# Linear attention with a SwiGLU feed-forward on one core: reordering batch 0's exponentials, cutting dummy matmuls, and merging batch 1's second products

## The chip, the cores and the metric

The kernel runs on one core of a Trainium2 chip. The metric is the device time of one execution in microseconds (us). Each kernel was executed several times; a time given alone is the median, with the lowest and highest beside it where they matter. The profile is one traced execution. Its "span" is 1.7 to 1.8 us shorter than the time of the same execution in every run of this study (315.0 us against a span of 313.2, 314.28 against 312.5). All runs quoted here are in the fast state.

## The reference

```python
def _attn_ref(q, k, v):                      # (8, 8, 576, 64) each: batch, head, sequence, head_dim
    def phi(x):
        return np.where(x > 0, x, np.exp(x) - 1.0) + 1.0
    q_p, k_p = (phi(q), phi(k))
    kv = np.einsum('bhsd,bhse->bhde', k_p, v)
    z = np.sum(k_p, axis=2)
    num = np.einsum('bhsd,bhde->bhse', q_p, kv)
    den = np.einsum('bhsd,bhd->bhs', q_p, z)[..., None] + 1e-06
    return num / den

def _moe_ref(x, w_gate, w_val, w_out):       # 4608 tokens, 512 -> 1536 -> 512
    g = x @ w_gate
    silu = g * (1.0 / (1.0 + np.exp(-g)))
    return (silu * (x @ w_val)) @ w_out
```

The attention's output, with the heads side by side, is the feed-forward's input x. The large work is the feed-forward, on PE (TensorE).

## The kernel before

Tokens are processed in periods of 512. One period is layer 1 (products with w_gate and w_val; two lines, L276 where the first chunks are taken in an order of their own, and L292 elsewhere) and layer 2 (products with w_out, L299). All operands are fp16, sums are fp32. Attention is hidden beside this, except for batch 0, which must be done before layer 1 can begin, and for the end of batch 1, which lies inside layer 2 of the first period.

Attention of one batch goes like this. phi of k is built as max(k, 0) + min(exp(k), 1): `exp_k` on ACT (ScalarE), `mx_k`, `mn_k` and `add_k` on DVE (VectorE). `q_exp` and `q_phi` do the same for batch 0's transposed q. `zt` sums phi(k) over the sequence on PE (L398), `zr_copy` spreads the sum, and `t_corners` with `Zr` is the q.z block (L254), the denominator. `lnrd` makes the reciprocal on ACT as exp(-ln). `kv_corner` is the product of phi(k) and v (L185), copied to `R`. `t_corners` with `R` is the q.R block (L254 again), the numerator. `x_t` multiplies numerator and reciprocal on DVE into `xT`, layer 1's input. A "dummy" (`warm`, L124) is a matmul on ones that nothing uses; it keeps PE active while it waits.

```python
WARM = (4, 1, 4, 5, 2, 1, 2, 2)              # how many dummies at each of eight places
...
def warm(n, w=512, ps=None):
    for _ in range(n):
        nc.tensor.matmul(out=(ps or pp4[1][1])[:, 512 - w:512], lhsT=ones[:, :],
                         rhs=ones[:, 0:1].to_broadcast([P, w]), start=True, stop=True)
...
# batch 0, cut: order of issue; each engine executes its own instructions in this order
q_turn(1, qb)                                # PE: transposes of q's second half
q_exp(1, 0, qb)                              # ACT
q_exp(1, 1, qb)                              # ACT
warm(WARM[2])
exp_k(0, 0)                                  # ACT
exp_k(0, 1)
q_phi(0, 0, qa)                              # DVE
q_phi(0, 1, qa)
mx_k(0, 0)
q_phi(1, 0, qb)
q_phi(1, 1, qb)
mn_k(0, 0)                                   # DVE, needs the first exp_k
zt(0, 0, X[1], kp, True, False)              # PE: z of half 0, part of max(k, 0)
warm(WARM[3])
zt(0, 0, X[1], ek, False, True)              # PE: z of half 0, part of min(exp(k), 1)
zr_copy(0, 0, X[1])
warm(WARM[4])
t_corners(0, Zr, 0, pp4[2])                  # PE: q.z block
lnrd(pp4[2], 0)                              # ACT: ln, exp
...
warm(WARM[6])
kv_corner(0, 0, kp, True, True)              # PE: products of v
...
warm(WARM[7], ps=pp4[2][1])
l1_mm(0, 0, pp4[2], (0,))                    # PE: first products of layer 1
l1_mm(0, 1, X, (0,))
t_corners(0, R, 1, pp4[1])                   # PE: second q.R block
x_t(0, 1, pp4[1])                            # DVE
...
# layer 2 of the first period, cut: its last part, with the end of batch 1
s4()                                         # den(0), den(1): q.z blocks and reciprocals of batch 1
for t in range(4):
    if t == 2:
        for lp in range(2):
            kv_corner(1, lp, kp, True, True)
        r_copy(1, 0, 2, "VV")
    if t == 3:
        nx(0, dz)                            # PE: q.R block, DVE: x_t
    for fb in range(FO, FB):
        l2_mm(0, t, fb)                      # PE: layer 2
    if t < 3:
        l2_out(0, t, "V")                    # DVE: copy of an output tile (L322)
nx(1, cq)
...
# layer 1 of the second period, cut
for cs in ((0, 1), (2, 3)):                  # chunks of x, two at a time
    for i in range(2):
        l1_mm(g, i, two[i], cs)
```

Of the kernel before, what the change touches and what calls it, by code (L numbers as in the profile page):

```python
# [9 lines left out]
AF = mybir.ActivationFunctionType  # L10
# [7 lines left out]
def kernel(  # L18
# [21 lines left out]
    EPS = 1e-6  # L40
    SC = 4096.0
    NB = 3
    WARM = (4, 1, 4, 5, 2, 1, 2, 2)

    sb = ctx.enter_context(tc.tile_pool(name="sb", bufs=1))
    pp = ctx.enter_context(tc.tile_pool(name="ps", bufs=1, space=bass.MemoryType.PSUM))
# [2 lines left out]
    def many(shape, dt, name, n=2):  # L49
        return [sb.tile(shape, dt, name=f"{name}_{i}") for i in range(n)]  # L50
# [12 lines left out]
    rd = many([P, 2, 512], FP16, "rd")  # L63

    q32 = sb.tile([P, HL, J * D], FP32, name="q32")
    lnt = many([P, 512], FP32, "lnt", 4)
# [19 lines left out]
    epsb = sb.tile([P, 1], FP32, name="epsb")  # L86
# [32 lines left out]
    def act(out, in_, func=AF.Copy, scale=1.0, bias=0.0):  # L119
        nc.scalar.activation(out=out, in_=in_, func=func, bias=bias, scale=scale)  # L120
# [5 lines that stand above are left out]
# [4 lines left out]
    def jl(t, b, lp):  # L130
        return t[b % 2][:, lp, :, :].rearrange("p j (l d) -> p l j d", d=D)

    def lj(t, b, lp):
        return t[b % NB][:, hs(lp), :].rearrange("p l (j d) -> p l j d", d=D)

    def exp_k(b, lp):
        act(jl(ek, b, lp), lj(kr, b, lp), AF.Exp)
# [4 lines left out]
    def mx_k(b, lp):  # L142
        nc.vector.tensor_scalar(out=jl(kp, b, lp), in0=lj(kr, b, lp), scalar1=0.0, scalar2=None, op0=ALU.max)

    def mn_k(b, lp):
        a = ek[b % 2][:, lp, :, :]
        nc.vector.tensor_scalar(out=a, in0=a, scalar1=1.0, scalar2=None, op0=ALU.min)  # L147
# [31 lines left out]
    def kv_corner(b, lp, t, first, last):  # L179
        ps = kvp[b]  # L180
        for j in range(J):
            for l2 in range(2):
                for hh in range(2):
                    rows = slice(C * hh, C * hh + C)
                    nc.tensor.matmul(out=ps[hh][D * l2:D * l2 + D, D * lp:D * lp + D],  # L185
                                     lhsT=t[b % 2][rows, lp, j, D * l2:D * l2 + D],
                                     rhs=vr[b % NB][rows, 2 * lp + l2, D * j:D * j + D],
                                     start=(first and j == 0), stop=(last and j == J - 1))
# [113 lines left out]
    def l2_open(g, t):  # L302
        if t % 2 == 0:
            l2p[(g, "p", t // 2)] = pair()
        l2p[(g, t)] = l2p[(g, "p", t // 2)][t % 2]
# [90 lines left out]
    def zt(b, lp, ps, t, first, last):  # L396
        for j in range(J):
            nc.tensor.matmul(out=ps[:, 0:2], lhsT=t[b % 2][:, lp, j, :], rhs=ob[:, 0:P:C],  # L398
                             start=(first and j == 0), stop=(last and j == J - 1))

    def zr_copy(b, lp, ps):
        nc.vector.tensor_scalar(out=Zr[b][:, lp, :, :], in0=ps[:, 0:2].unsqueeze(2).to_broadcast([P, 2, D]),
                                scalar1=1.0 / SC, scalar2=None, op0=ALU.mult)

    def lnrd(ps, i, w0=0, w1=512, early=False):
        for l2 in range(2):
            act(lnt[2 * i + l2][:, w0:w1], ps[l2][:, w0:w1], AF.Ln, bias=epsb[:, 0:1])
            if not early:
                act(rd[i][:, l2, w0:w1], lnt[2 * i + l2][:, w0:w1], AF.Exp, scale=-1.0)
        for l2 in range(2 if early else 0):  # L410
            act(rd[i][:, l2, w0:w1], lnt[2 * i + l2][:, w0:w1], AF.Exp, scale=-1.0)

    def xmul(dst, ps, r):
        nc.vector.scalar_tensor_tensor(out=dst, in0=ps, scalar=1.0 / SC, in1=r, op0=ALU.mult, op1=ALU.mult)

    def x_t(g, lp, ps, l2s=(0, 1)):
        for l2 in l2s:
            xmul(xT[g % 2][:, 2 * lp + l2, :], ps[l2][:, :], rd[lp][:, l2, :])

    def t_corners(g, W, lp, ps):  # L420
        for (b, j0, j1, c0) in units(g)[1]:
            corners(ps, W[b], b, lp, j0, j1, c0)

    def q_one(pair_):
        for h in range(2):
            nc.tensor.matmul(out=pair_[h][:, :], lhsT=part[:, :], rhs=ones[:, 0:1].to_broadcast([P, 512]),
                             start=True, stop=False)

    def q_turn(lp, pair_):
        for l2 in range(2):  # L430
            for j in range(J - 1):
                nc.tensor.matmul(out=pair_[j // 4][D * l2:D * l2 + D, P * (j % 4):P * (j % 4) + P],
                                 lhsT=qr[0][:, 2 * lp + l2, D * j:D * j + D], rhs=id16[:, :],
                                 start=False, stop=(j % 4 == 3))

    def q_half(lp, h):
        return qT[0][:, lp, 4 * h:4 * h + 4, :, :].rearrange("p j h c -> p (j h c)")

    def q_exp(lp, h, pair_):
        act(q_half(lp, h), pair_[h][:, :], AF.Exp, bias=m1[:, 0:1])  # L440

    def q_phi(lp, h, pair_):
        a = q_half(lp, h)
        nc.vector.scalar_tensor_tensor(out=a, in0=pair_[h][:, :], scalar=1.0, in1=a, op0=ALU.max, op1=ALU.min)  # L444

    kvp[0] = pp4[1]
    X = [pp4[0][0], pp4[3][0]]
    Y = [pp4[3][1], pp4[0][1]]
    qa, qb = pp4[2], pp4[0]
# [3 lines left out]
    nc.vector.tensor_copy(out=qr[0][:, 3, :], in_=q32[:, 3, :])  # L453
    warm(WARM[0])
    q_one(qa)
# [3 lines left out]
    q_exp(0, 1, qa)  # L459
    warm(WARM[1])  # L460
    q_turn(1, qb)
    q_exp(1, 0, qb)
    q_exp(1, 1, qb)
    warm(WARM[2])
    exp_k(0, 0)
    exp_k(0, 1)
    q_phi(0, 0, qa)
    q_phi(0, 1, qa)
    mx_k(0, 0)
    q_phi(1, 0, qb)  # L470
    q_phi(1, 1, qb)
    mn_k(0, 0)
    zt(0, 0, X[1], kp, True, False)
    warm(WARM[3])
    zt(0, 0, X[1], ek, False, True)
    zr_copy(0, 0, X[1])
    warm(WARM[4])
    t_corners(0, Zr, 0, pp4[2])
    lnrd(pp4[2], 0)
    mx_k(0, 1)  # L480
    mn_k(0, 1)
    zt(0, 1, Y[0], kp, True, False)
    warm(WARM[5])
    zt(0, 1, Y[0], ek, False, True)
# [6 lines left out]
    r_copy(0, 0, 1, "VV")  # L491
    add_k(0, 1)
    t_corners(0, R, 0, X)
    x_t(0, 0, X, (0,))
    kv_corner(0, 1, kp, True, True)
    x_t(0, 0, X, (1,))
    r_copy(0, 1, 2, "VV")
    warm(WARM[7], ps=pp4[2][1])
    l1_mm(0, 0, pp4[2], (0,))
# [20 lines left out]
    def p1_open():  # L520
        b1p["z"] = kvp[1] = pair()
        ring.pop()
        b1p["q"] = pair()
        ring.pop()
# [54 lines left out]
    def layer2_0():  # L579
        for t in range(4):  # L580
            l2_open(0, t)
        p1_open()
        cq, dz = b1p["q"], b1p["z"]
        nc.scalar.preload_act_table_set("natural_log_exp_and_others")

        def den(lp, ps):
            t_corners(1, Zr, lp, ps)
            lnrd(ps, lp, early=(lp == 0))

        def nx(lp, ps):  # L590
            t_corners(1, R, lp, ps)
            x_t(1, lp, ps)

        def s0():
            act(eq[0][:, :, D * 8:D * 9], qr[0][:, :, D * 8:D * 9], AF.Exp)
            exp_k(1, 1)
            exp_q(1, 0)
            exp_q(1, 1)
            phi_q8()
            mx_p(0)  # L600
            mn_k(1, 1)
            add_k(1, 1)
            mn_q(1, 0)
            add_p(0)
            mx_p(1)
            mn_q(1, 1)
            add_p(1)

        def s1():
            turn(0, cq[0])  # L610

        def s3():
            turn(1, cq[1])
            for b in range(2):
                for lp in range(2):
                    turn8(b, lp, dz[0])
            p1_z()
            for b in range(2):
                copy8(b, dz[0])

        def s4():
            den(0, dz)
            den(1, cq)

        step = {1: [s0], 6: [s1], 8: [s3]}
        FO = 9
        for fb in range(FO):
            for f in step.get(fb, []):
                f()
            for t in range(4):  # L630
                l2_mm(0, t, fb)
        s4()
# [4 lines that stand above are left out]
                r_copy(1, 0, 2, "VV")  # L637
            if t == 3:
                nx(0, dz)
            for fb in range(FO, FB):  # L640
                l2_mm(0, t, fb)
            if t < 3:
                l2_out(0, t, "V")
        nx(1, cq)
        exp_k(2, 0)
        exp_k(2, 1)
        l2_out(0, 3, "V")
        exp_q(2, 0)
        exp_q(2, 1)
        phi_k(2, 0)  # L650
        phi_k(2, 1)
        ring[:] = [l2p[(0, "p", 0)], dz, cq, l2p[(0, "p", 1)]]
# [112 lines left out]
```

## Time and profile before

| | before |
|---|---|
| time, median of 3 | 315.43 us (315.13 to 315.48) |
| the profiled execution | 315.0 us, span 313.2 us |
| PE busy | 307.0 us, 98% of the span |
| batch 0: second q.R block starts | 15.92 us |
| layer 2 of the first period starts | 36.17 us |
| L292 of the second period starts | 54.08 us |

The first row and the second differ: the profiled execution was the fastest that was seen of this kernel at that point. This will matter. The last three rows are marks in the one stream of work that never stops afterwards: whatever moves them moves the end. The lines of this profile are shown and read in the prediction. A line of the chain of waits there has start (us), duration (us), engine, the tile written, the source line and the number of instructions joined in that piece. A timeline line has start, duration, engine, line, operation, output and inputs with shapes and types, and in brackets the idle time before and what ended it.

### The profile page before, as it was taken

Reading aid. Unit: us, or ns where it says so; the run is one execution under the profiler, and the core shown is the slowest. Engines: PE = TensorE matmul, PEld = TensorE weight load, DVE = VectorE, ACT = ScalarE, POOL = GpSimd, SP = SyncE. Lnnn points to the kernel's source line nnn. Section 1 sums busy time; section 2 is a strip of 40 time slices with the busy share of each in tenths; the row PEclk is TensorE's granted clock in tenths of the full one; section 3 lists DMA queues with packets and bytes.
Section 4 is the critical chain, followed back from the end, with each engine's and each line's share of the span. In section 5 each row is a group of like instructions: output and inputs, shape, how many; then the busy total and the mean of one; then the engine's idle time right before and its main releaser. Section 6 shows DMA issues by size and latency. Waiting matters only on the chain.

```text
span 313.2 us, 5502 instructions
## 1 busy us (share of the span) xinstructions
PE 307.0 (98%) x2173; PEld 142.7 (46%) x2173; DVE 203.8 (65%) x361; ACT 154.0 (49%) x232; POOL 46.9 (15%) x72
## 2 busy tenths in 40 slices
PE   7999999999999999999999999999999999999994
PEld 3444454444544454445444544444444444444442
DVE  4854859899799667977697849874991434143410
ACT  4855869739633745365535743475330333133311
POOL 8645344300000410004000500000000000000000
PEclk9999999999999999999999999999999999999999
DMA  8999999997612494149912990314032300140014
GB/s 217 194 197 200 206 206 235 236 207 106 130 33 41 80 191 129 38 40 137 226 30 46 127 236 1 75 40 96 2 67 58 87 1 1 40 97 0 0 36 100
DMA packets 41162, 32.80 MB, mean 105 GB/s; under 512 B 16432, under 2 KB 36144, under 8 KB 41136
## 3 DMA queue, kind: packets, MB, share of 16 engines
q0 software_dynamic: 20464, 18.29, 37.3%
q1 hardware_dynamic: 20592, 14.13, 19.6%
q8 instruction: 17, 0.28, 0.4%
q14 instruction: 9, 0.07, 0.1%
q10 hardware_dynamic: 80, 0.03, 0.0%
HBM read 37.75 MB, written 9.44 MB: 151 GB/s over the span
## 4 chain that ended last, share of the span: by engine, by line
PE 95%; DVE 2%; DMA 1%; SPq 0%; issue 0%; ACT 0%
PE pp L292 57%; PE pp L299 30%; PE pp L276 2%; PE pp L254 2%; PE pp L185 2%; DMA q<-in_q_dram 1%; DVE qT L444 1%; PE pp L124 1%; PE pp L398 0%; PE pp L370 0%; DVE kp L159 0%; PE pp L212 0%; DVE osb L322 0%; DVE ek L147 0%; SPq L333 0%; DVE qr L452 0%
## 5 line engine op out<-in xcount | busy, mean ns | idle before, releaser
L120 ACT ACTIVATE sil<-pp 128x512 f16<-128x512 f32 x108 | 63.4, 597 | 101.6 <-PE pp L292 95.2
L292 PE MATMUL pp<-xT,wg 128*128 128x512 f16 x416 | 106.8, 379 | 0.0
L292 PE MATMUL pp<-xT,wv 128*128 128x512 f16 x416 | 106.8, 379 | 0.0
L285 DVE SCALAR_TENSOR_TENSOR hT<-pp,sil 128x512 f16<-128x512 f32 x108 | 72.3, 680 | 49.1 <-PE pp L292 35.5
L299 PE MATMUL pp<-wo,hT 128*128 128x512 f16 (+2 forms) x444 | 97.1, 373 | 0.6 <-DVE osb L322 0.6
L299 PEld LDWEIGHTS <-hT 128*128 128x128 f16 x444 | 42.0, 98 | 49.8 <-issue 2.1
L292 PEld LDWEIGHTS <-wv 128*128 128x128 f16 x416 | 40.7, 98 | 49.1
L292 PEld LDWEIGHTS <-wg 128*128 128x128 f16 x416 | 40.7, 98 | 48.4
L322 DVE TENSOR_SCALAR osb<-pp 128x512 f32<-128x512 f32 (+1 forms) x19 | 12.9, 682 | 30.8 <-PE pp L299 30.8
L120 ACT ACTIVATE osb<-pp 128x512 f32<-128x512 f32 (+1 forms) x18 | 10.3, 574 | 34.8 <-PE pp L299 34.8
L120 ACT ACTIVATE ek<-kr 128x1152 f16<-128x1152 f16 x16 | 17.8, 1154 | 0.1
L120 ACT ACT_TABLE_LOAD x13 | 16.7, 1283 | 2.3 <-PE pp L292 2.1
L229 DVE TENSOR_TENSOR qp<-qp,rden 128x1152 f16<-128x1152 f16 x12 | 16.2, 1347 | 0.0
L220 DVE TENSOR_REDUCE den<-prod 128x18 f32<-128x1152 f16 x12 | 16.1, 1341 | 0.0
L120 ACT ACTIVATE eq<-qr 128x1152 f16<-128x1152 f16 (+1 forms) x15 | 15.9, 1099 | 0.3 <-DMA qr<-in_q_dram 0.3
L696 POOL COPY gate<-qT 128x1 f16<-128x1 f16 x4 | 0.7, 186 | 97.4 <-DMA qT<-qp 97.4
L271 DVE TENSOR_SCALAR xT<-pp 128x512 f16<-128x512 f32 (+1 forms) x14 | 8.8, 666 | 7.1 <-PE pp L254 7.1
L103 POOL DMA_DIRECT2D kr<-in_k_dram x16 | 11.6, 725 | 9.5 <-DMA vr<-in_v_dram 3.4
L103 POOL DMA_DIRECT2D vr<-in_v_dram x16 | 11.6, 728 | 8.3 <-PE pp L292 2.5
L159 DVE TENSOR_TENSOR kp<-ek,kp 128x1152 f16<-128x1152 f16 x16 | 12.1, 758 | 0.5
L147 DVE TENSOR_SCALAR ek<-ek 128x1152 f16<-128x1152 f16 x16 | 7.5, 470 | 5.4 <-ACT ek L120 5.4
L103 POOL DMA_DIRECT2D qr<-in_q_dram x14 | 10.0, 714 | 6.3 <-DMA wo<-in_moe_w_out_dram 1.8
(82 smaller groups left out, 180.9 us busy)
## 6 DMA issues: line engine op xcount, KB each, us to landing
out_dram<-osb SPq DMA_DIRECT2D x70, 128.0 KB, 3.5
kr<-in_k_dram POOLq DMA_DIRECT2D x16, 288.0 KB, 8.9
vr<-in_v_dram POOLq DMA_DIRECT2D x16, 288.0 KB, 9.8
qr<-in_q_dram POOLq DMA_DIRECT2D x14, 288.0 KB, 12.1
wo<-in_moe_w_out_dram POOLq DMA_DIRECT2D x3, 512.0 KB, 13.0
wg<-in_moe_w_gate_dram POOLq DMA_DIRECT2D x5, 256.0 KB, 9.5
wv<-in_moe_w_val_dram POOLq DMA_DIRECT2D x5, 256.0 KB, 10.1
q<-in_q_dram SPq DMA_DIRECT2D x2, 576.0 KB, 4.1
```

Source lines behind the costliest of these rows:

```text
L103: nc.gpsimd.dma_start(out=dst[b % NB][:, 2 * lp:2 * lp + 2, :], in_=src[b].rearrange("(l a) (c j) d -> (a c) l (j d)", a=2, j=J)[:, 2 * lp ...
L120: nc.scalar.activation(out=out, in_=in_, func=func, bias=bias, scale=scale)
L147: nc.vector.tensor_scalar(out=a, in0=a, scalar1=1.0, scalar2=None, op0=ALU.min)
L159: nc.vector.tensor_tensor(out=a, in0=ek[b % 2][:, lp, :, :], in1=a, op=ALU.add)
L185: nc.tensor.matmul(out=ps[hh][D * l2:D * l2 + D, D * lp:D * lp + D], lhsT=t[b % 2][rows, lp, j, D * l2:D * l2 + D], rhs=vr[b % NB][rows, 2 ...
L220: nc.vector.tensor_reduce(out=den[:, c, :], in_=prod[:, :, :].rearrange("p j (l d) -> p (j l) d", d=D), axis=AX.X, op=ALU.add)
L229: nc.vector.tensor_tensor(out=qv, in0=qv, in1=rden[:, c, :].unsqueeze(2).to_broadcast([P, 2 * J, D]), op=ALU.mult)
L271: nc.vector.tensor_scalar(out=dst, in0=ps[l2][:, c0:], scalar1=1.0 / SC, scalar2=None, op0=ALU.mult)
L285: nc.vector.scalar_tensor_tensor(out=hT[g % 2][:, fb, :], in0=ps[1][:, :], scalar=SC, in1=s[:, :], op0=ALU.mult, op1=ALU.mult)
L292: nc.tensor.matmul(out=ps[h][:, :], lhsT=w[:, c, P * fb:P * fb + P], rhs=xT[g % 2][:, c, :], start=(c == 0), stop=(c == 3))
L299: nc.tensor.matmul(out=l2p[(g, t)][:, n0:n1], lhsT=hT[g % 2][:, fb, P * t:P * t + P], rhs=wo[:, fb, n0:n1], start=(fb == 0), stop=(fb == F ...
L322: nc.vector.tensor_scalar(out=o[:, n0:n1], in0=ps[:, n0:n1], scalar1=1.0 / SC, scalar2=None, op0=ALU.mult)
```

## The change

In batch 0, the first exp of k goes between the two exps of q's second half, so that z can begin earlier; q's last min/max moves behind the copy of z; and four dummies go (two of five ahead of z's second products, one of two ahead of v's first, one of two ahead of layer 1). In batch 1, all four logs go ahead of the four exps on ACT, and both q.R blocks become one block of 16 products ahead of the last output tile of layer 2. The two calls of `x_t(0, 0, ...)` become one around `kv_corner`, which does not alter the order on any engine.

```diff
--- before.py
+++ after.py
@@ -40,7 +40,7 @@
     EPS = 1e-6
     SC = 4096.0
     NB = 3
-    WARM = (4, 1, 4, 5, 2, 1, 2, 2)
+    WARM = (4, 1, 4, 3, 2, 1, 1, 1)
 
     sb = ctx.enter_context(tc.tile_pool(name="sb", bufs=1))
     pp = ctx.enter_context(tc.tile_pool(name="ps", bufs=1, space=bass.MemoryType.PSUM))
@@ -402,12 +402,9 @@
         nc.vector.tensor_scalar(out=Zr[b][:, lp, :, :], in0=ps[:, 0:2].unsqueeze(2).to_broadcast([P, 2, D]),
                                 scalar1=1.0 / SC, scalar2=None, op0=ALU.mult)
 
-    def lnrd(ps, i, w0=0, w1=512, early=False):
+    def lnrd(ps, i, w0=0, w1=512):
         for l2 in range(2):
             act(lnt[2 * i + l2][:, w0:w1], ps[l2][:, w0:w1], AF.Ln, bias=epsb[:, 0:1])
-            if not early:
-                act(rd[i][:, l2, w0:w1], lnt[2 * i + l2][:, w0:w1], AF.Exp, scale=-1.0)
-        for l2 in range(2 if early else 0):
             act(rd[i][:, l2, w0:w1], lnt[2 * i + l2][:, w0:w1], AF.Exp, scale=-1.0)
 
     def xmul(dst, ps, r):
@@ -460,16 +457,16 @@
     warm(WARM[1])
     q_turn(1, qb)
     q_exp(1, 0, qb)
+    exp_k(0, 0)
     q_exp(1, 1, qb)
     warm(WARM[2])
-    exp_k(0, 0)
     exp_k(0, 1)
     q_phi(0, 0, qa)
     q_phi(0, 1, qa)
     mx_k(0, 0)
     q_phi(1, 0, qb)
-    q_phi(1, 1, qb)
     mn_k(0, 0)
+    mx_k(0, 1)
     zt(0, 0, X[1], kp, True, False)
     warm(WARM[3])
     zt(0, 0, X[1], ek, False, True)
@@ -477,7 +474,7 @@
     warm(WARM[4])
     t_corners(0, Zr, 0, pp4[2])
     lnrd(pp4[2], 0)
-    mx_k(0, 1)
+    q_phi(1, 1, qb)
     mn_k(0, 1)
     zt(0, 1, Y[0], kp, True, False)
     warm(WARM[5])
@@ -491,9 +488,8 @@
     r_copy(0, 0, 1, "VV")
     add_k(0, 1)
     t_corners(0, R, 0, X)
-    x_t(0, 0, X, (0,))
+    x_t(0, 0, X)
     kv_corner(0, 1, kp, True, True)
-    x_t(0, 0, X, (1,))
     r_copy(0, 1, 2, "VV")
     warm(WARM[7], ps=pp4[2][1])
     l1_mm(0, 0, pp4[2], (0,))
@@ -585,7 +581,8 @@
 
         def den(lp, ps):
             t_corners(1, Zr, lp, ps)
-            lnrd(ps, lp, early=(lp == 0))
+            for l2 in range(2):
+                act(lnt[2 * lp + l2][:, :], ps[l2][:, :], AF.Ln, bias=epsb[:, 0:1])
 
         def nx(lp, ps):
             t_corners(1, R, lp, ps)
@@ -621,6 +618,8 @@
         def s4():
             den(0, dz)
             den(1, cq)
+            for i in range(4):
+                act(rd[i // 2][:, i % 2, :], lnt[i][:, :], AF.Exp, scale=-1.0)
 
         step = {1: [s0], 6: [s1], 8: [s3]}
         FO = 9
@@ -637,11 +636,11 @@
                 r_copy(1, 0, 2, "VV")
             if t == 3:
                 nx(0, dz)
+                nx(1, cq)
             for fb in range(FO, FB):
                 l2_mm(0, t, fb)
             if t < 3:
                 l2_out(0, t, "V")
-        nx(1, cq)
         exp_k(2, 0)
         exp_k(2, 1)
         l2_out(0, 3, "V")
```

> **What bounds the kernel now.** I read the page first, then the list of waits of PE over the whole run, then the chain of waits for the first 75 us, then the timeline around the two places that the diff touches. Part 1 of the page:
>
> ```profile
> PE 307.0 (98%) x2173; PEld 142.7 (46%) x2173; DVE 203.8 (65%) x361; ACT 154.0 (49%) x232; POOL 46.9 (15%) x72
> ```
>
> PE is busy for 307.0 of 313.2 us. Its longest waits, in the list of waits of PE:
>
> ```profile
> PE pp L124 <- DVE ones L355: 1.1, 1, 1.1
> PE pp L299 <- DVE osb L322: 0.6, 1, 0.6
> PE pp L432 <- DVE qr L452: 0.3, 1, 0.3
> ```
>
> The first is the start, the second is the end, the third is q's arrival. From 19 us to 308 us PE never stands still: the chain there is layer 1 and layer 2 back to back, and each period's 96 products of L292 take 20.72 us, 215.8 ns apiece. So only two things can move the end: the time at which the stream of layer 1 begins (batch 0's start-up, where a busy PE is partly dummies), and PE work or stalls inside the stream (batch 1's part). A microsecond saved at the start is a microsecond at the end, unless a transfer takes over. The chain of waits in the start-up:
>
> ```profile
> 7.95 0.45 DVE kp L143
> 8.41 1.20 DVE qT L444 x2
> 9.60 0.01 issue
> 9.61 0.47 DVE ek L147
> 10.09 0.05 issue
> 10.13 0.39 PE pp L398 x9
> ...
> 12.12 0.45 PE pp L124 x2
> 12.57 0.48 PE pp L185 x36
> ...
> 14.11 0.48 PE pp L185 x36
> 14.59 0.54 PE pp L124 x2
> 15.13 0.86 PE pp L276 x4
> 15.99 0.34 PE pp L254 x4
> 16.33 2.74 PE pp L276 x12
> ```
>
> The reader should see DVE's min of exp(k) at 9.61 (L147), which lets z's products go at 10.13, and dummies (L124) directly on the path at 12.12 and at 14.59. The timeline says what holds 9.61: the exp of k's first half is on ACT from 8.42, behind both exps of q's second half, and one such exp lasts 1.16 us, so it ends at 9.58.
>
> ```profile
> 7.27 1.27 ACT L120 ACTIVATE qT<-pp,m 128x512 f16<-128x512 f32 x2 [0.39 <-PE pp L432]
> 8.42 2.21 ACT L120 ACTIVATE ek<-kr 128x1152 f16<-128x1152 f16 x2
> ```
>
> **What the Trainium skill says.** "Perfetto Trace Analysis", Per-engine timelines: ACT and DVE are strict FIFO, and the end of a matmul is a modelled time. The trace agrees with the first: k's first half landed by 7.94 (issued at 1.34, 6.6 us to landing), yet its exp starts only at 8.42. "ScalarE: Activation LUTs", What ACT_TABLE_LOAD costs: back-to-back ACTIVATEs overlap by about 93 ns. Here a log of 0.69 us lets an independent successor start after 0.58, but its own exp only after 0.72, so alternating costs about 0.13 per pair. "TensorEngine Tiling (Array Packing)", Key Properties: a change of tiling mode drains TensorE. Here the 64x64 block at 15.92 starts 0.09 after the slot that the 216 ns pitch would give it, and the weight loads ahead of such blocks show 0.42 of idle. "TensorE: Matmul & The Clock Gate", Part 1: idle PE loses its clock after about 3.4 us. The granted clock is 1.00 in every stretch that I asked for, and no PE gap near the removed dummies reaches 0.5 us, so I expect nothing from that.
>
> **The change, part by part.** *Exp of k between q's exps.* The first q exp starts at 7.27 and frees ACT at 7.85; k is there at 7.94 (DVE's first max of k, at 7.95, was waiting for it too). So the exp of k runs 7.95 to 9.11 instead of 8.42 to 9.58: 0.47 earlier. It pushes q's last exp to 9.00 and k's second exp to 9.57 to 10.73, 0.10 later. On DVE the order becomes: max k0, q's third min/max (8.32 to 9.00), min k0 at 9.14, max k1 at 9.52, then q's fourth min/max only after the copy of z. The min of k0 thus ends at 9.60 instead of 10.07. The dummies ahead of it on PE must not be in the way: they start at 8.71, so five of them issue until 9.79, which would block a start at 9.66; three until 9.36, which does not. That is what the cut from 5 to 3 buys. z's products then start at 9.66 instead of 10.13, the copy of z at 10.09 (before 10.56), the q.z block at 10.44 (10.91), the first log at 10.88 (11.35; ACT is free at 10.73). All 0.47 earlier.
>
> *The second half of k and the dummies.* DVE: q's fourth min/max 10.30 to 10.97, min k1 10.89 to 11.35 (before 11.13 to 11.58), add k0 11.26 to 12.01 (before 11.50 to 12.25). Only 0.24 is left of the gain here. But v's first products began at 12.50 although add k0 was done at 12.25: two dummies stood in front. With one dummy they start at 12.10, at the add plus 0.06 to 0.09: 0.40 earlier. The copies of R, add k1 and v's second products follow 0.40 earlier (13.71 against 14.11). The first xT multiply goes from 13.97 to 13.57. The last dummies: layer 1's first product is at 14.97, behind two dummies issued from 14.52, while its input ended at 14.64. With one dummy from 14.13 the product starts at 14.35, its input being ready at 14.30: 0.62 earlier. The four products end their issue at 15.21, the second q.R block starts at 15.30 (before 15.92; R's copies end at 15.11, so they do not hold it).
>
> *The last link* is the multiply on DVE:
>
> ```profile
> 16.44 1.29 DVE L414 SCALAR_TENSOR_TENSOR xT<-pp,rd 128x512 f16<-128x512 f32 x2 [0.92 <-ACT rd L120]
> ```
>
> The view names ACT as releaser. Each of the two multiplies waits only for its own half, though, and the first one's reciprocal was done near 15.2; 16.44 is the end of the q.R block (16.33) plus 0.11. I choose PE as the cause. Then this multiply moves to 15.83 and the third chunk of layer 1 from 17.18 to 16.56. The fourth reciprocal, at 15.95 after the shift of 0.47, is in time for the second multiply at 16.42. Gain: 0.62.
>
> *Batch 1.* Four logs first: the first reciprocals end later (48.98 for 47.80), the last earlier (50.56 for 50.79). The two q.R blocks become one: two small blocks took 0.35 and 0.40 us on the chain, the undivided q.z block of the same 16 products 0.64, and one refill of about 0.1 goes: about 0.2 to 0.27 of PE time. But what follows is held by DVE:
>
> ```profile
> 49.13 0.69 DVE L322 TENSOR_SCALAR osb<-pp 128x512 f32<-128x512 f32 x1 [0.18 <-PE pp L299]
> 49.73 2.47 DVE L414 SCALAR_TENSOR_TENSOR xT<-pp,rd 128x512 f16<-128x512 f32 x4
> 51.07 0.10 PEld L276 LDWEIGHTS <-wv 128*128 128x128 f16 x1 [0.22 <-issue]
> ```
>
> The multiplies stand behind the output copy of 49.13, which waits for PE and does not move against it. They are 0.60 apart, so chunk 1 of layer 1 cannot start before the second one's end, 51.00, plus 0.06, which is where it starts now. PE reaches chunk 0 at about 50.25 and waits at chunks 0 and 1. I count 0.0 here, at most 0.05.
>
> *Sum:* 0.62 + 0.0, taken from 315.43, is 314.81.
>
> **The rivals.** (a) *A transfer takes over.* An earlier stream meets fixed landings. Next wv block: 9.64 + 9.1 = 18.74, needed at 19.55 now, at 18.93 after: 0.19 left. Second w_out block: 25.77 + 13.0 = 38.77, needed at 36.17 + 16 x 0.216 = 39.62, after the shift 39.00: 0.23 left. q's second half of batch 1 at 40.2: with its exp, min and add the transposes are ready at about 42.73, needed at 42.96. All hold, narrowly, and each caps the gain at about 0.8. A landing 0.3 late would make it about 0.5: 314.9 to 315.0. (b) *The multiply waits for all reciprocals*, as the page names it: ACT's four pairs of log and exp move by 0.47 only, so 0.45: 314.98. (c) *DVE takes the gain:* it now has q's fourth min/max in the path of k1, and loses 0.23 of the 0.47 there; if dummies were not the binding thing at 12.50 and 14.97, about 0.25 remains: 315.2. For it: modelled PE ends blur 0.05 to 0.1. Against it: three starts fit the dummies' pitch. (d) *The merged block pays in full*, 0.2 more: 314.6. Against it stands the start of chunk 1 at a DVE end. (e) *Fewer dummies cool the clock:* products of twice the length for microseconds, 316 or more. The granted clock speaks against it.
>
> **Range and chances.** The sum gives 314.81; (a), (b) and (c) are likelier than (d), so I put the middle at 314.9. The runs of before spread over 0.35 us (315.13 to 315.48), as much as the differences among the rivals. 314.4 to 315.3 covers these and the spread. Two per cent is 6.3 us; start-up holds only some 2 us of PE idleness, so no route leads there: faster 0.005, same 0.985, slower 0.01 for (e).
>
> **What would show it.** Right: exp of k at 7.95, its min at 9.14, z's products at 9.66, v's products at 12.10 and 13.71, layer 1's first product at 14.35, the second q.R block at 15.30, the multiply at 15.83 (rather than 16.0, which is rival b); layer 2 of the first period, now at 36.17, starting near 35.55; and between layer 2 and chunk 1 of batch 1 the same distance as before (36.17 to 51.06, 14.89 us) with a PE stall at chunks 0 and 1. Wrong: a wait of PE for wv, w_out or qp between 19 and 44 us; a distance shorter than 14.7 us (rival d); a granted clock under 1.

## The result, and the profile after

| | before | after | moved by |
|---|---|---|---|
| time, median of 4 each, same chip | 315.46 (315.13 to 315.49) | 314.34 (314.26 to 314.43) | 1.12 |
| span of the profiled execution | 313.2 | 312.5 | 0.7 |
| second q.R block starts | 15.92 | 15.29 | 0.63 |
| layer 2 of the first period starts | 36.17 | 35.54 | 0.63 |
| L292 of the second period starts | 54.08 | 53.46 | 0.62 |

The ratio of the times is 0.9967, with a 95% interval of 0.995 to 0.9984; by the margin of 2% the verdict is "same". Ratios here are the mean time of one kernel's fast runs over that of the other's of the same rounds, so they are not quite the ratio of the medians quoted.

The gain that the trace shows, 0.63 us, is there by 15.3 us and is kept to the end. Busy time by engine, part 1 of the page of the changed kernel:

```profile
PE 306.2 (98%) x2169; PEld 142.3 (46%) x2169; DVE 204.0 (65%) x361; ACT 153.9 (49%) x232; POOL 47.4 (15%) x72
```

PE has four instructions fewer, the four dummies, and 0.8 us less busy time. Its share stays at 98%: busy work that nobody needs went, and the span went with it.

The chain of waits of the changed kernel in the start-up, in the same columns as in the prediction:

```profile
7.97 1.17 ACT ek L120
9.14 0.02 issue
9.17 0.47 DVE ek L147
...
9.69 0.39 PE pp L398 x9
...
11.81 0.24 PE pp L124
...
12.09 0.55 PE pp L185 x36
...
13.70 0.48 PE pp L185 x36
14.18 0.32 PE pp L124
14.50 0.86 PE pp L276 x4
15.36 0.34 PE pp L254 x4
```

Compare it with the chain in the prediction. The exp of k (`ek`, L120) is now on the chain itself, from 7.97, and DVE's min follows at 9.17, where it was 9.61. z's products (L398) start at 9.69, where they were at 10.13. The pairs of dummies (`L124 x2`) at 12.12 and 14.59 have become single ones, and v's first products (L185) start at 12.09, where they started at 12.50.

The timeline of the changed kernel for the exp of k, the q exp behind it, and the last multiply:

```profile
7.97 1.16 ACT L120 ACTIVATE ek<-kr 128x1152 f16<-128x1152 f16 x1
9.04 0.67 ACT L120 ACTIVATE qT<-pp,m 128x512 f16<-128x512 f32 x1
...
15.81 1.29 DVE L411 SCALAR_TENSOR_TENSOR xT<-pp,rd 128x512 f16<-128x512 f32 x2 [0.70 <-PE pp L254]
```

The first two lines show the new order on ACT. The third names PE's q.R block as what the multiply waited for. In the kernel before the same view had named ACT.

In batch 1 the chain of waits of the changed kernel reads:

```profile
48.46 0.62 PE pp L254 x16
...
49.11 0.69 DVE xT L411
...
49.84 0.59 PE pp L276 x2
...
50.44 3.18 PE pp L276 x14
```

And the timeline of DVE in the same stretch:

```profile
48.50 0.69 DVE L322 TENSOR_SCALAR osb<-pp 128x512 f32<-128x512 f32 x1 [0.18 <-PE pp L299]
49.11 2.47 DVE L411 SCALAR_TENSOR_TENSOR xT<-pp,rd 128x512 f16<-128x512 f32 x4
```

The q.R block is one piece of 16 products now. But DVE is on the chain behind it: the output copy (L322) runs from 48.50, and the multiplies can start only at 49.11. Two products of layer 1 (`x2`) take 0.59 us instead of the 0.43 that two at 0.216 take, since PE waits for the next multiply. The starts of PE's products give the size of both waits, beside a later run (x_first_chunks_again, below) in which PE does not wait here. From the start of the last three products of layer 2 to chunk 0 it took 0.88 us (48.96 to 49.84), there 0.70; from chunk 0 to chunk 1 it took 0.60, there 0.43. So PE stood still for about 0.18 us ahead of chunk 0 and 0.17 ahead of chunk 1.

### The profile page after: what moved, and what is told of

Its sections match the earlier page's. It is cut to its first block, busy times and chain, and to the rows that moved or that the text cites. A ratio compares the mean times of both kernels' runs of the same rounds, so it can differ in the third digit from the quotient of the medians.

```text
span 312.5 us, 5494 instructions
## 1 busy us (share of the span) xinstructions
PE 306.2 (98%) x2169; PEld 142.3 (46%) x2169; DVE 204.0 (65%) x361; ACT 153.9 (49%) x232; POOL 47.4 (15%) x72
## 4 chain that ended last, share of the span: by engine, by line
PE 95%; DMA 1%; DVE 1%; ACT 1%; issue 0%; SPq 0%; DVEq 0%
PE pp L292 57%; PE pp L299 30%; PE pp L276 2%; PE pp L254 2%; PE pp L185 2%; DMA q<-in_q_dram 1%; PE pp L124 0%; ACT ek L120 0%; PE pp L398 0%; PE pp L370 0%; PE pp L429 0%; DVE xT L411 0%; ACT qT L120 0%; DVE kp L159 0%; PE pp L212 0%
## 5 line engine op out<-in xcount | busy, mean ns | idle before, releaser
L120 ACT ACTIVATE sil<-pp 128x512 f16<-128x512 f32 x108 | 63.4, 597 | 101.8 <-PE pp L292 100.0
L292 PE MATMUL pp<-xT,wg 128*128 128x512 f16 x416 | 106.8, 379 | 0.0
L292 PE MATMUL pp<-xT,wv 128*128 128x512 f16 x416 | 106.8, 379 | 0.0
L292 PEld LDWEIGHTS <-wv 128*128 128x128 f16 x416 | 40.7, 98 | 49.1
L292 PEld LDWEIGHTS <-wg 128*128 128x128 f16 x416 | 40.7, 98 | 48.4
L322 DVE TENSOR_SCALAR osb<-pp 128x512 f32<-128x512 f32 (+1 forms) x19 | 12.9, 682 | 30.9 <-PE pp L299 26.5
L120 ACT ACTIVATE osb<-pp 128x512 f32<-128x512 f32 (+1 forms) x18 | 10.3, 574 | 34.8 <-PE pp L299 34.8
L120 ACT ACTIVATE ek<-kr 128x1152 f16<-128x1152 f16 x16 | 17.9, 1157 | 0.1
L120 ACT ACTIVATE eq<-qr 128x1152 f16<-128x1152 f16 (+1 forms) x15 | 16.0, 1102 | 0.1
```

The costliest lines, as they stand in the source:

```text
L120: nc.scalar.activation(out=out, in_=in_, func=func, bias=bias, scale=scale)
L292: nc.tensor.matmul(out=ps[h][:, :], lhsT=w[:, c, P * fb:P * fb + P], rhs=xT[g % 2][:, c, :], start=(c == 0), stop=(c == 3))
L322: nc.vector.tensor_scalar(out=o[:, n0:n1], in0=ps[:, n0:n1], scalar1=1.0 / SC, scalar2=None, op0=ALU.mult)
```

## The experiments

Three sets ran, each on one chip, and each with its own executions of the kernel before: the first set had 315.21 us for it (314.94 to 315.79, 9 runs), the second 315.35 (315.13 to 315.65, 11 runs), the third 315.29 (314.92 to 317.02, 11 runs; one odd execution of 317.02 still counts as fast, raises the mean of before and widens this set's intervals).

One kernel's executions differ by as much as the whole effect. So beside the times I use distances inside the traces. These are the marks in the start-up (us):

| run | q's first 16 transposes take | first max of k starts | z's second products | v's first products | second q.R block | from max of k to z | from z to q.R |
|---|---|---|---|---|---|---|---|
| before | 0.89 | 7.95 | 10.13 | 12.50 | 15.92 | 2.18 | 5.79 |
| before_again | 1.26 | 7.95 | 10.14 | 12.51 | 15.93 | 2.19 | 5.79 |
| batch1_only | 1.23 | 8.37 | 10.45 | 12.82 | 16.24 | 2.08 | 5.79 |
| late_q_before | 0.89 | 8.22 | 10.47 | 12.84 | 16.26 | 2.25 | 5.79 |
| dummies_only | 1.50 | 8.02 | 10.51 | 12.68 | 15.88 | 2.49 | 5.37 |
| order_only | 1.50 | 7.87 | 9.80 | 12.43 | 15.85 | 1.93 | 6.05 |
| no_dummies | 1.49 | 8.29 | 9.96 | 12.37 | 16.42 | 1.67 | 6.46 |
| after | 0.89 | 7.97 | 9.69 | 12.09 | 15.29 | 1.72 | 5.60 |
| after_again | 0.89 | 8.46 | 10.18 | 12.59 | 15.79 | 1.72 | 5.61 |
| batch0_only | 1.50 | 8.02 | 9.74 | 12.14 | 15.34 | 1.72 | 5.60 |
| late_q_after | 1.50 | 8.25 | 10.16 | 12.57 | 15.77 | 1.91 | 5.61 |
| x_first_chunks | 0.89 | 8.20 | 9.91 | 12.31 | 15.52 | 1.71 | 5.61 |
| x_first_chunks_two_blocks | 1.31 | 7.86 | 9.54 | 11.94 | 15.14 | 1.68 | 5.60 |
| x_first_chunks_again | 0.89 | 7.85 | 9.53 | 11.94 | 15.14 | 1.68 | 5.61 |

The max of k waits for k's landing or for DVE, whichever is later, and starts anywhere from 7.85 to 8.46. The last column hardly moves within one kind of kernel: 5.79 in all four that have before's start-up, 5.60 or 5.61 in all seven that have after's.

### The kernel before, again

No edit. It shows the spread.

> The kernel before, unchanged, run again for its spread and a second trace. The trace of before at hand belongs to its fastest execution (315.0 us, span 313.2), while its other runs took 315.13 to 315.49. Theory A (the gain is the 0.63 us seen in the traces, and the rest of the measured 1.1 us is a spread of before that its profiled run didn't show): times between 315.0 and 315.5, ratio 1.000; the spans differ by as much as the times, and a slower trace shows where, most likely in transfers landing later in the first 20 us. Theory B (the change gains something that the trace does not show): every run of before is at 315.4 or above with a span of 313.6, and the trace at hand was the odd one.

Measured: 315.33 us (314.95 to 315.59, 5 runs), ratio 1.0003 (0.999 to 1.0016). The same kernel spreads over 0.64 us here, and the spans of the executions (313.2 to 313.8) follow their times. The execution that was traced was again a fast one, 315.0 us. So a difference of a few tenths between two medians says little, and one profile of before is not its median. Theory B, which had every run of before at 315.4 or above, is out.

### Batch 1's part alone

```diff
 # the kernel before, with
-            lnrd(ps, lp, early=(lp == 0))
+            for l2 in range(2):
+                act(lnt[2 * lp + l2][:, :], ps[l2][:, :], AF.Ln, bias=epsb[:, 0:1])
 ...
             den(1, cq)
+            for i in range(4):
+                act(rd[i // 2][:, i % 2, :], lnt[i][:, :], AF.Exp, scale=-1.0)
 ...
                 nx(0, dz)
+                nx(1, cq)
 ...
-        nx(1, cq)
```

> Before with the change of batch 1 alone (four logs first, both q.kv blocks as one). My theory: 0.0, at most 0.05 us faster, because chunk 1 of layer 1 waits for the second xT multiply on DVE (51.06 before); PE reaches chunk 0 about 0.25 us earlier and stands still that long at chunks 0 and 1. Rival d: the merged block pays 0.2 us or more in the total, and 51.06 becomes 50.8.

Measured: 315.20 us (314.86 to 315.82), ratio 1.0003 (0.999 to 1.0015). From the start of layer 2 to L292 of the second period it took 17.97 us, 0.06 of which is a wait at batch 1's transposes; before took 17.91. The stall at chunk 1 is there as in the changed kernel (two products in 0.59 us, then fourteen in 3.18). Batch 1's part is worth nothing by itself, and the rival that it pays 0.2 falls.

### Batch 0's part alone

The edit is the reverse of the last one, made on the changed kernel.

```diff
 # the changed kernel, with
+                if lp == 1:
+                    act(rd[lp][:, l2, :], lnt[2 * lp + l2][:, :], AF.Exp, scale=-1.0)
+            for l2 in range(2 if lp == 0 else 0):
+                act(rd[lp][:, l2, :], lnt[2 * lp + l2][:, :], AF.Exp, scale=-1.0)
 ...
-            for i in range(4):
-                act(rd[i // 2][:, i % 2, :], lnt[i][:, :], AF.Exp, scale=-1.0)
 ...
-                nx(1, cq)
 ...
+        nx(1, cq)
```

> The changed kernel with batch 1 as before: exps of k and q interleaved and the fewer dummies alone. My theory: the whole gain, so the same time as the changed kernel (314.3 to 314.4) and third chunk of layer 1 at 16.55, first product of layer 2 at 35.54. Rival d: 0.2 us or more slower than the changed kernel.

Measured: 314.59 us (314.39 to 315.13), ratio 0.9988 (0.9974 to 1.0002); the median lies 0.62 under that of before in the same set. The trace has the second q.R block at 15.34 (15.29 in the changed kernel) and 17.91 us from layer 2 to the second L292. The whole of the traced gain is batch 0's. The time is 0.2 above the 314.3 to 314.4 that was expected; the changed kernel did not run in this set, so the two were not compared on one chip.

### Fewer dummies alone

```diff
 # the kernel before, with
-    WARM = (4, 1, 4, 5, 2, 1, 2, 2)
+    WARM = (4, 1, 4, 3, 2, 1, 1, 1)
```

> Before with the smaller numbers of dummies alone, the order of the exps as before. My theory, from the timeline of before: z's products stay at 10.13 (the min of exp k still ends at 10.07), v's first products start 0.19 earlier (12.31, at the end of add k0 plus 0.06), layer 1's first product 0.42 earlier (14.55), the q.R block at 15.50, the third chunk at 16.76: 0.42 us faster. Rival: the dummies keep PE's clock up or only fill waits, so taking them away gains nothing (under 0.1 us) and the whole 0.62 is the order's.

Measured: 315.20 us (314.87 to 315.51), ratio 1.0001 (0.9988 to 1.0013): nothing in the time. A gain of 0.42 would be a ratio of 0.9987, just outside that interval. The trace says more. From z's second products to the second q.R block it took 5.37 us where before takes 5.79: 0.42 was gained, as expected. But q's first transposes took 1.50 us in this execution instead of 0.89, the q exp and all behind it came 0.37 later, and so z started 0.38 later. A further 0.21 went at batch 1's transposes near 41 us (0.62 us of PE time for the usual 0.50), and the timeline says how:

```profile
38.58 0.72 POOL L103 DMA_DIRECT2D qr<-in_q_dram  x1 [1.80 <-DMA wo<-in_moe_w_out_dram]
...
38.88 0.67 DVE L147 TENSOR_SCALAR ek<-ek 128x1152 f16<-128x1152 f16 x1
```

DVE's min took 0.67 us, though it takes 0.46 nearly everywhere. It started 0.30 us after POOL began to issue a DMA. The last section comes back to this. So in the execution that was traced, two losses covered what the cut of dummies brings. Whether the other four lost it in the same way, no trace shows. The stretched min at this place is not rare: order_only, no_dummies and late_q_after have it too (0.64 to 0.69 us), so in 4 of the 14 traces.

### The new order alone

```diff
 # the changed kernel, with
-    WARM = (4, 1, 4, 3, 2, 1, 1, 1)
+    WARM = (4, 1, 4, 5, 2, 1, 2, 2)
```

> The changed kernel with the old numbers of dummies (5, 2, 1, 2, 2 from the fourth on). My theory, from the changed kernel's timeline: five dummies hold z's second products until 9.82 when they began at 8.74 (0.13 later than now), two hold v's first products until 12.30 (0.21 later), two hold layer 1's first product until 14.76 (0.42 later). So the order alone is worth 0.20 us: second q.R block 7.22 us after z's first products (changed kernel 6.80, before 7.46). Rival: dummies only fill waits, and this is as fast as the changed kernel.

Measured: 315.09 us (314.68 to 315.14), ratio 0.999 (0.9978 to 1.0002); the median is 0.26 under before's, and 0.20 was expected. In this one trace next to nothing is gained. From the max of k to the second q.R block it takes 7.98 us (1.93 and 6.05), and 7.97 in before. From z's first products, the mark that the expectation named, it takes 7.37, where before has 7.46 and 7.22 was expected. Two things of this execution go with the shortfall. The transposes of q took 1.50 us, and with them PE came later to z's first products (0.61 us after the max of k; 0.52 in the changed kernel) and to the five dummies behind them: z's second products came at 1.93, where the expectation has 1.85 (9.82 less 7.97). And two DVE instructions on the chain took 0.65 and 0.57 instead of 0.46 while POOL was issuing a DMA: from z to the second q.R block it took 6.05, where the expectation has 5.89 (15.71 less 9.82). After the start-up, another 0.23 went at batch 1's transposes, as in dummies_only. So the share of 0.20 rests on the median, whose interval includes none, and on the difference between dummies_only's 0.42 and the whole.

### No dummies in the stretch at all

```diff
 # the changed kernel, with
-    WARM = (4, 1, 4, 3, 2, 1, 1, 1)
+    WARM = (4, 1, 4, 0, 0, 0, 0, 0)
```

> The changed kernel without any dummy from the fourth number on (0, 0, 0, 0, 0). My theory: each of these waits now ends with DVE and not with a dummy, so 0.04 us faster at most, 6.75 us from z's first products to the second q.R block, and layer 1's products stay 0.216 apart. Rival e (dummies keep the clock up): products of layer 1 about twice as far apart for 1 to 3 us, 1 us or more slower in the total.

Measured: 315.98 us (315.24 to 316.92, 6 runs), ratio 1.0025 (1.001 to 1.0039): the gain is gone, and the median is 0.63 over before's of the same set. My theory, which had it at most slightly faster, fell here; the rival of the cooled clock was right for this kernel. The view of stretches of the changed kernel comes first, then that of this one (from:to, length, then busy us and count of PE, PEld, DVE, ACT, POOL, then the granted clock, the DMA share and GB/s):

```profile
8.00:12.00 4.00, 3.80 (x49) 1.57 (x47) 3.75 (x9) 3.83 (x5) 2.24 (x3) 1.00 1.26 200
12.00:16.00 4.00, 3.59 (x92) 1.71 (x92) 2.91 (x10) 3.89 (x8) 3.47 (x5) 1.00 1.44 195
```

```profile
8.00:12.00 4.00, 2.60 (x44) 1.50 (x42) 3.78 (x9) 3.83 (x6) 2.15 (x3) 1.00 1.23 197
12.00:16.00 4.00, 3.35 (x88) 1.61 (x84) 3.00 (x9) 3.91 (x7) 3.35 (x6) 0.71 1.45 195
```

PE was busy 2.60 of the 4 us from 8 to 12, and in the next stretch the granted clock was 0.71. Asked for narrower stretches, the same view gives 1.00 from 10.29 to 13.70 us, with PE busy for 2.40 of the 3.41, and 0.50 from 13.70 to 17.11. In all six executions the mean clock was lower (0.989 to 0.995) than in any run of the other kernels (0.997 or more), and the three with 0.989 were the slowest. The timeline of PE shows two of layer 1's first products, and the longest wait ahead of them:

```profile
9.96 0.39 PE L398 MATMUL pp<-ob,ek 128*128 128x2 f16 x9 [0.78 <-DVE ek L147]
...
15.01 0.63 PE L276 MATMUL pp<-xT,wv 128*128 128x512 f16 x1
15.43 0.63 PE L276 MATMUL pp<-xT,wg 128*128 128x512 f16 x1
```

The products are 0.42 us apart, twice the 0.216 of everywhere else, until about 17 us. No single wait was longer than 0.78 us. z came at 1.67 us after the max of k, as early as in the changed kernel; the 0.85 us of difference between 6.46 and 5.61 all lies behind it. So the dummies that were kept earn their place, and the change cut them to a number that still holds the clock: the changed kernel's executions have 3.28 to 3.86 us of PE work between 8 and 12, and 1.00 of clock.

### The changed kernel, again

No edit, in the second set.

> The changed kernel unchanged, for its spread beside nine or so runs of before. Theory: executions differ in the first 8 us (q's transposes took 0.89 to 1.50 us for sixteen in the traces so far, k's first half landed between 7.4 and 8.4), so times spread over 0.5 us or more here too: 314.2 to 314.9 with a median near 314.5, 0.5 to 0.8 below before. Rival B (a gain that the trace does not show): all runs at 314.2 to 314.45, 1 us below before. In the trace: 6.8 us from z's first products to the second q.R block, where before has 7.35 to 7.47.

Measured: 314.44 us (314.21 to 314.96, 5 runs), ratio 0.9974 (0.9962 to 0.9986). The median is 0.91 under before's. Its traced execution was the slowest of the five, because k landed late and the exp of k started at 8.46; from there on it took 1.72 and 5.61 us, as in the first trace.

### q held back, in both kernels

The medians of the first comparison differ by 1.12 us and the traces by 0.63. One theory for the rest: in executions in which q comes late, before loses more, since its exp of k stands behind both exps of q. The same cast of q, done twice in both kernels, makes q late without any other change.

```diff
 # the kernel before (late_q_before) and the changed kernel (late_q_after), with
-    nc.vector.tensor_copy(out=qr[0][:, 2, :], in_=q32[:, 2, :])
+    for _ in range(2):
+        nc.vector.tensor_copy(out=qr[0][:, 2, :], in_=q32[:, 2, :])
```

> Before with the cast of q's third head done twice on DVE, so that q's second half reaches ACT about 0.38 us late, as it does in the executions whose transposes run slowly. Theory C (the measured gain exceeds the 0.63 of the first two traces because a late q costs the old order more): both exps of q, then k's, move by 0.38; z's second products at 10.51 where they were at 10.13, second q.R block 7.46 us after k's max allowed z's first products plus that lateness (near 16.30 for a k landed at 7.95): 0.3 to 0.4 us slower than before. Rival: k's landing governs, and the total stays within 0.1.

> The changed kernel with the same doubled cast. Theory C: only q's third exp stands ahead of k's, and it had 0.12 us to spare before k landed; so k's exp starts at 8.23 and z's second products at 9.95 where they were at 9.69: 0.26 us slower than the changed kernel, and 0.12 less than the old order loses. The gap between the two late kernels is then about 0.75. Rival: the new order loses as much, 0.38, and the gap stays 0.63; then a late q explains nothing of the excess.

Measured: 315.57 us (315.35 to 315.86) with the order of before, 314.87 (314.44 to 315.31) with that of after; ratios 1.0007 (0.9989 to 1.0024) and 0.9984 (0.9966 to 1.0002). The medians are 0.70 apart. In before, z's second products came at 10.47 (expected 10.51) and the second q.R block at 16.26 (16.30). In after they came at 10.16, where 9.95 was expected. The exp of k was on time at 8.22, but then the timeline shows:

```profile
9.11 0.74 POOL L112 DMA_DIRECT2D wv<-in_moe_w_val_dram  x1 [0.80 <-DMA kr<-in_k_dram]
...
9.41 0.70 DVE L147 TENSOR_SCALAR ek<-ek 128x1152 f16<-128x1152 f16 x1
```

The min took 0.70 for 0.46, again 0.30 us after the start of a POOL issue: that is the missing 0.2. Without it the traces' q.R blocks would be 0.73 apart, not the 0.49 (16.26 less 15.77) that they are. The theory asked for a gap well above 0.63 in the times, and 0.70 does not bear it out.

### Multiplies ahead of the output copy, chunks one by one

Batch 1's merged block brought nothing because DVE's output copy stands ahead of the multiplies. Here it goes behind them, and layer 1 of the second period takes its chunks one at a time, so that each is needed as late as possible.

```diff
 # the changed kernel, with
                 nx(0, dz)
                 nx(1, cq)
+                l2_out(0, 2, "V")
 ...
-            if t < 3:
+            if t < 2:
                 l2_out(0, t, "V")
 ...
-                    for cs in ((0, 1), (2, 3)):
+                    for cs in ((0,), (1,), (2,), (3,)):
```

> The changed kernel with two further edits in batch 1: the output copy of the third tile goes behind the four xT multiplies on DVE, and layer 1 of the second group takes its chunks one at a time for both blocks (0,0,1,1,2,2,3,3 and not 0,1,0,1,2,3,2,3). My theory (the multiplies hold PE after the merged block): the first multiply starts when its products are there, about 0.25 us earlier, PE never waits at chunks 0 and 1, and the stream from chunk 1 on comes 0.40 us earlier: from the first product of layer 2 of the first period (35.54) to the first L292 product of the second (53.46), 17.92 us become 17.52; 0.4 us faster than the changed kernel in the total. Rival: something else holds it (the four exps, PSUM), and it gains under 0.1 us.

> x_first_chunks again, for a firmer time of the version that should beat both: the stage from layer 2 to L292 again 17.56 us, a median near 314.15, ratio to before 0.9965 (0.63 from the start and 0.35 from batch 1, of 315.3, give 0.9969; the excess seen so far is 0.2 more).

Measured: 314.30 us (313.82 to 314.71), ratio 0.9967 (0.9955 to 0.9979) in the second set, and 314.09 (313.80 to 314.30), ratio 0.9958 (0.9941 to 0.9975) in the third. From layer 2 to the second L292 both traces have 17.56 us; 17.52 was expected and 17.91 is what before and after have. The chain of waits of the second one:

```profile
48.31 0.56 PE pp L254 x16
48.88 0.76 PE pp L299 x3
49.63 3.49 PE pp L276 x16
```

No DVE piece is left in it: the last three products of layer 2 follow the q.R block and all sixteen products of layer 1 follow those, in 3.49 us or 0.218 apiece. DVE's multiplies now start right behind the block:

```profile
48.76 2.48 DVE L411 SCALAR_TENSOR_TENSOR xT<-pp,rd 128x512 f16<-128x512 f32 x4 [0.59 <-PE pp L254]
```

That is 13.37 us after the start of layer 2 (35.39); in the changed kernel it was 13.57 (49.11 less 35.54). The two edits did not run apart. An estimate from these marks gives about 0.20 of the 0.35 us to the copy, the earlier start of the multiplies, and the rest to the order of the chunks.

### The same, with the two q.R blocks apart

```diff
 # x_first_chunks, with
                 nx(0, dz)
-                nx(1, cq)
-                l2_out(0, 2, "V")
 ...
+        nx(1, cq)
+        l2_out(0, 2, "V")
```

> x_first_chunks, but with q.R of batch 1 in two blocks again (logs still first). My theory: once DVE's multiplies no longer hold PE, the undivided block does pay: from layer 2's first product of the first period to the first L292 product of the second 17.76 us where x_first_chunks has 17.56 and both before and the changed kernel 17.91. Rival: the two blocks cost nothing even then, 17.56 again.

Measured: 314.29 us (314.13 to 314.63), ratio 0.9967 (0.9948 to 0.9987). The stage takes 17.76 us, as expected: 0.20 more than with the merged block. So the merging does save the 0.2 us of PE time that the prediction counted, once nothing else holds the same place.

x_first_chunks is the best version that ran. Against before it gains 1.05 us by the medians of the second set and 1.20 by those of the third. Against the changed kernel the traces give it 0.35 us; the only comparison of the two times on one chip, 314.30 against 314.44 with five runs each, has overlapping ranges and does not show it.

## Why the prediction was right, and what in it was not

**Exp of k and z: right.** The steps were expected at 7.95, 9.14 and 9.66 and came at 7.97, 9.17 and 9.69. The q.z block came at 10.46 (10.44), the first log at 10.90 (10.88). The table of marks gives this part as 0.46 us (2.18 less 1.72), and five traces with after's start-up repeat it within 0.05 where no DVE instruction was stretched.

**DVE and the dummies: right.** The gain of 0.47 was to shrink to 0.24 on DVE and to come back as dummies go: v's first products at 12.10, layer 1's first product at 14.35, the second q.R block at 15.30. Measured: 12.09, 14.34 and 15.29. In dummies_only 0.42 of it comes with the dummies alone, in before's order, by the distance from z to the second q.R block; the time of dummies_only does not show it. The new order's own 0.20 is the difference, which the times of order_only fit but its trace does not show. So the whole of 0.63 is shown, and its split between order and dummies is only argued.

**The last link: right, and rival (b) wrong.** The multiply starts at 15.81 (15.83 expected, about 16.0 under the rival), and the view now names PE's block as what released it. It also starts before the last reciprocal ends (15.34 to 15.97 on ACT), so it cannot have waited for all of them. In before the view had put it down to ACT: the last reciprocal ended at 16.42 there, just ahead of 16.44, but it belongs to the second multiply, and the first one's had been done at 15.18.

**Batch 1: right, and rival (d) wrong as stated.** 0.0 was expected; the stage took 17.91 before and 17.92 after, and batch1_only agrees. The reason given, a DVE that holds the multiplies behind an output copy, was tested from the other side: moving the copy and the chunks freed 0.35 us in all, as much as PE had stood still at chunks 0 and 1 (0.18 and 0.17), and the merged block's 0.20 appeared.

**Rival (a), a transfer: wrong.** No trace has a wait of PE for wv or w_out. The 0.06 to 0.2 us that some executions lose at batch 1's transposes come through DVE, in dummies_only through an instruction stretched beside a POOL issue, not through a landing. **Rival (c)**, which left about 0.25, is wrong: the starts that fit the dummies' pitch moved with the dummies. **Rival (e)** was wrong for the cut as made and right for taking all of them away.

**What failed: the term it was all subtracted from, and the shading.** The shift was 0.63 where 0.62 was predicted. But "taken from 315.43, is 314.81" subtracts a difference of traces from a median. The traced execution had taken 315.0 us; 315.0 less 0.63 is 314.37, and the changed kernel's median came out at 314.34. That these two agree to 0.03 is partly luck: before's own medians differ by more from set to set (315.21 to 315.46), and the changed kernel's second one is 314.44. Then the middle was raised to 314.9 for rivals (a), (b) and (c), none of which held. The median thus lies 0.06 us below the low end of the range, 314.4. The range took its lower side as if only the mechanism could move it, and gave the starting point's own spread too little room below.

**What stays open.** Medians on one chip put the gain at 1.12 us (the first comparison), 0.91 (after_again), 0.62 (batch0_only) and 0.70 (the pair with late q), and the traces at 0.63. A gain of 0.63, a ratio of 0.998, lies inside the intervals of the first comparison, of after_again and of batch0_only. So the excess in some of them may be chance. The medians of the parts (0.01 for the dummies, 0.26 for the order, 0.01 for batch 1) do not add up to the whole either. That late q is its cause was tested and not borne out; nothing else that I tried shows a cause.

## What to carry to other kernels

When a stream of work never stops after its start, find the one chain that starts it and check at each link what PE itself has queued ahead: an earlier input is worth only what the filler in front of it lets through, and filler can be cut down but not away without watching the granted clock. A saving on one engine shows only if the next link waits for that engine; batch 1's 0.2 us of PE time was real, but lay behind a copy on DVE until the copy and the order of the chunks were changed. For effects under a microsecond, subtract traces from traces and medians from medians, and measure distances between marks inside the trace.

## What the Trainium skill lacked or had wrong

- "TensorE: Matmul & The Clock Gate", the table in "Why this matters for your kernels", warns of gaps of PE longer than about 3 us between bursts. In no_dummies no gap was longer than 0.78 us, yet with 2.60 us of PE work in the 4 us before, the granted clock fell to 0.71 in the next 4 us (0.50 from 13.70 to 17.11) and products came 0.42 us apart instead of 0.216. With 3.28 us of work or more in the same stretch it stayed at 1.00. Many short gaps do it too. The page's part on a second failure mode does tell of such a kernel, but gives no share of work at which it begins; where the limit lies between 2.60 and 3.28, these runs do not show.
- The same page says that the moment at which the clock is let go varies from run to run, and the runs agree: q's first 16 transposes took 0.89, 1.23 to 1.31 or 1.50 us. The first clock record in the packed traces goes with it, run by run: it stands at 3.7 to 4.9 us in the six traces with 0.89, at 5.6 to 5.8 in the three with 1.23 to 1.31, and at 6.5 to 7.0 in the five with 1.49 or 1.50. What no page says is that before this record the profile's granted clock reads 1.00: in before, from 0 to 3 us and from 3 to 6, although its first eight products (1.06 to 4.65 us) lie about 0.43 us apart, twice the 0.216 of later, and its record starts at 4.67. The column did not show the slow start; the distances did.
- "SBUF — State Buffer", "Who interferes with whom", says that a DVE instruction in a two-port mode and a GpSimd instruction lock each other out, the first one to issue holding the ports for its whole instruction. The traces agree in kind, in both directions, but not with "whole" for a DMA issue on POOL, which lasts about 0.72 us. The 14 traces have 192 DVE min and max instructions of 128x1152 fp16 that start during such an issue. The 50 that start 0.27 to 0.48 us after the issue's start are all stretched, so that they end as if they had begun at 0.50 to 0.57 (0.67 us at 0.30, 0.57 at 0.40). The 85 that start at up to 0.26 are not stretched, and the POOL issue then takes up to 0.95 us.
- No page says how far apart executions of one kernel on one core lie when nothing is wrong: before went from 314.94 to 315.79 us within one set, with k's max starting anywhere from 7.85 to 8.46 us across the traces.
